# Taking pk^T x over contiguous feature chunks, with z regrouped through memory

## The chip, the cores and the metric

One core of one Trainium2 chip runs the whole program. The metric is the device time of one execution in microseconds (us). Executions of one kernel mostly agree within 1%; much of the scatter comes from the first loads, which let TensorE begin its real work up to some 3 us earlier or later. So beside the whole time I use a stretch that leaves the beginning out: from the start of the first matmul of pk^T x to the end of the last matmul, read from the trace. There is one trace of each kernel.

In the code, `sb(...)` allocates on-chip memory (SBUF), `PS` is the memory that TensorE writes its results to (PSUM), and `nc.dram_tensor` lies in memory outside the core, which the text calls memory. A DMA has landed when its completion is signalled.

## The reference

Two linear-attention blocks A and B work on the same x (2048 x 640, 32 heads of 20 features). A gate mixes their outputs.

```python
def _A_ref(x, wqkv, wo):                 # B is the same with its own weights
    qkv = ...                            # x @ wqkv, split into q, k, v by head
    phi = lambda t: jnp.where(t > 0, t + 1, jnp.exp(t)) + 1e-6
    pq, pk = phi(q), phi(k)
    kv = jnp.einsum("bhsd,bhse->bhde", pk, v)
    z = jnp.einsum("bhsd->bhd", pk)
    num = jnp.einsum("bhqd,bhde->bhqe", pq, kv)
    den = jnp.einsum("bhqd,bhd->bhq", pq, z)[..., None] + 1e-6
    o = num / den
    return ... @ wo
x = A_x
g = _sigmoid((x * gate_w).sum(-1, keepdims=True))
return g * a + (1 - g) * b               # a, b: the two blocks
```

## The kernel before

It never forms v. It computes G = pk^T x, then G wv, masks that to the diagonal blocks of the heads, and folds the result with wo into one matrix per block (WP), which is applied to the scaled pq at the end. z comes from a column of ones that is appended to x: the last column of pk^T [x 1] is the sum of pk over the rows.

Features f are later held in the grouping f = 5 i + k (partition i, group k). To get G and z in that grouping for free, the weights of a matmul of group k are every fifth column of pk:

```python
XW = 642                                  # row length of XN: 640 + the ones column, padded by 1
XN = sb("XN", [128, NT, XW])              # x, row tile t holds rows 128 t to 128 t + 127
...
def g_unit(X, k):                         # X is "A" or "B", k = 0..4
    for t in range(NT):                   # 16 row tiles
        w = PK[X][:, t, k : D : NC]       # stride 5 elements = 10 bytes
        r.append((PS[:, tile.banks[0], 0:HALF], w, XN[:, t, 0:HALF], t == 0, t == NT - 1, None))
        r.append((PS[:, tile.banks[1], 0 : HALF + 1], w, XN[:, t, HALF : D + 1], t == 0, t == NT - 1, None))
    ...
    # z: one column of the second bank, already grouped modulo 5
    e.tensor_copy(Z32[X][:, k : k + 1], PS[:, tile.banks[1], HALF : HALF + 1])
    # G goes to GT by a transposing DMA

def zbd(X):                               # z times the head mask: weights of the denominator
    e.tensor_tensor(out=ZBD[X][:, :, :], in0=<head mask>, in1=Z32[X] broadcast, op=ALU.mult)

def m_unit(X, w):                         # G wv by blocks of 120 columns, then the mask on VectorE
    e.tensor_tensor(
        out=MB[...].rearrange("p q (i k) -> p q k i", k=NC),      # scattered write
        in0=PS[...].rearrange("p (q k i) -> p q k i", ...), in1=<mask>, op=ALU.mult)
...
den: PS[32 rows, 0:256] += ZBD[X][:, k, :] x PQ[X][:, k, ...]     # needs ZBD of A and B, and all pq of the block of rows
```

All instructions are laid out ahead of time by a list scheduler inside the kernel's program. It uses its own estimates of durations and fixes the order of each engine; at run time each engine executes its order and waits where an operand isn't there. For a DMA the estimate is the `us=` argument plus 2 us.

## Time and profile before

| what | value |
|---|---|
| time, median of 3 runs | 200.29 us (199.82 to 201.01) |
| span of the profiled run | 198.6 us |
| TensorE busy, clock | 97%, full throughout |
| first pk^T x matmul to last matmul | 51.60 to 195.55 = 143.95 us |

The first fence holds lines of the page: busy time by engine, then, over 40 equal slices of the span, TensorE's busy tenths and the clock that it was granted. PE is TensorE, PEld its weight loads, DVE VectorE, ACT ScalarE, SP the queue that issues most DMAs.

```profile
span 198.6 us, 3244 instructions
PE 191.7 (97%) x1373; PEld 133.0 (67%) x1379; DVE 105.5 (53%) x201; ACT 79.5 (40%) x124; POOL 6.0 (3%) x16
...
PE   7699999999999999999999999999999999999993
...
PEclk9999999999999999999999999999999999999999
```

TensorE is the bound: it is busy for nine tenths or more of every slice but the first two and the last. Next come groups of instructions by shape: engine, operation, out<-in, count | busy us, mean ns of one | idle before.

```profile
L393 PE MATMUL ps<-XN,FEA 128*128 128x320 bf16 x80 | 22.2, 300 | 0.0
L393 PEld LDWEIGHTS ps<-XN,FEA 128*128 128x128 bf16 x160 | 18.8, 117 | 3.4
...
L393 PEld LDWEIGHTS ps<-WKA,XT 128*128 128x128 bf16 x160 | 15.5, 98 | 5.9
...
L598 DVE TENSOR_TENSOR MB<-ps,CB 120x480 bf16<-120x480 f32 x2 | 3.0, 1507 | 0.1
...
L598 DVE TENSOR_TENSOR MB<-ps,CB 120x120 bf16<-120x120 f32 x2 | 1.2, 583 | 0.0
...
L598 DVE TENSOR_TENSOR MB<-ps,CB 40x40 bf16<-40x40 f32 x2 | 0.5, 261 | 0.1
```

A strided weight load takes 117 ns, a contiguous one 98. The mask (MB) takes about 2.35 us a block (1.51 + 0.58 + 0.26). The table of windows shows how busy each engine is (columns: length; busy us and count of PE, PEld, DVE, ACT, POOL; clock; share of the DMA engines; GB/s), and VectorE's timeline shows z's product:

```profile
107.00:112.00 5.00, 5.00 (x35) 3.01 (x34) 4.60 (x10) 2.89 (x5) 0.00 (x0) 1.00 0.47 168
112.00:118.00 6.00, 5.92 (x62) 3.92 (x61) 5.87 (x11) 3.02 (x6) 0.00 (x0) 1.00 0.00 0
118.00:125.00 7.00, 6.94 (x35) 3.80 (x34) 6.97 (x15) 5.72 (x11) 0.00 (x0) 1.00 0.26 54
```

```profile
100.95 0.15 DVE L552 COPY ZB<-ps 128x1 f32<-128x1 f32 x1
101.13 0.33 DVE L563 TENSOR_TENSOR ZBDB<-CB,ZB 128x160 bf16<-128x160 bf16 x1
```

z of B is complete at 101.1 us and multiplied at once. The first denominator, which needs it, starts at 113.93. VectorE works nearly all the time after that, but TensorE is idle for only 0.14 of these 18 us.

Last, the only DMA of 640 separate small elements (two bytes each) in this trace, the load of the gate vector (issue to landing in us at the end of the line):

```profile
GWC<-in_gate_w_dram SPq DMA_DIRECT2D x1, 1.2 KB, 2.9
```

### The profile page before, as it was taken

To read this page: it belongs to the slowest core of one execution; us is meant where nothing else is said; L and a number is where in the kernel's file an instruction comes from. 1 tells how busy PE (TensorE), PEld (TensorE's weight loads), DVE (VectorE), ACT (ScalarE), POOL (GpSimd) and SP (SyncE) were. 2 spreads that over 40 slices of the span, in tenths; PEclk is the share of its full clock that TensorE was granted. 3 is DMA by queue.
4 is the path that set the end of the run, shared out by engine and by line. 5 is a ranking of instruction groups with operands and counts; after the bars stand their busy time and mean duration, and the time that the engine had idled before them with its cause. 6 is when DMAs were issued, how large, how long until landed. Compare 5 with 4: busy or idle time off the path is not lost.

```text
span 198.6 us, 3244 instructions
## 1 busy us (share of the span) xinstructions
PE 191.7 (97%) x1373; PEld 133.0 (67%) x1379; DVE 105.5 (53%) x201; ACT 79.5 (40%) x124; POOL 6.0 (3%) x16
## 2 busy tenths in 40 slices
PE   7699999999999999999999999999999999999993
PEld 2467777777788877888855655455766665566772
DVE  0359888888600000041159999999405369961400
ACT  2055455455311128302255378545233155514221
POOL 5000000000000000500000000000000000000000
PEclk9999999999999999999999999999999999999999
DMA  6999999990011411111135302440110210011021
GB/s 179 307 232 142 282 348 248 293 224 13 3 33 33 36 33 33 36 33 33 38 80 139 144 0 46 122 165 3 45 54 33 69 61 7 0 36 66 33 69 66
DMA packets 26754, 18.96 MB, mean 95 GB/s; under 512 B 15860, under 2 KB 26484, under 8 KB 26740
## 3 DMA queue, kind: packets, MB, share of 16 engines
q1 hardware_dynamic: 26020, 17.94, 35.5%
q10 hardware_dynamic: 720, 0.82, 1.5%
q8 instruction: 11, 0.18, 0.4%
q14 instruction: 3, 0.02, 0.0%
HBM read 10.89 MB, written 4.26 MB: 76 GB/s over the span
## 4 chain that ended last, share of the span: by engine, by line
PE 93%; DMA 3%; ACT 1%; DVE 1%; issue 1%; SPq 0%
PE ps L393 93%; DMA XN<-in_A_x_dram 3%; DVE FEA L506 0%; SPq L382 0%; PE ps L471 0%; ACT EK L497 0%; ACT OS L808 0%; DVE EK L501 0%
## 5 line engine op out<-in xcount | busy, mean ns | idle before, releaser
L497 ACT ACTIVATE EK<-ps 128x640 bf16<-128x640 f32 x32 | 22.3, 703 | 25.9 <-PE ps L393 25.8
L701 ACT ACTIVATE EK<-ps 128x512 bf16<-128x512 f32 x40 | 23.9, 598 | 19.0 <-PE ps L393 19.0
L808 ACT ACTIVATE OS<-ps 128x640 bf16<-128x640 f32 x16 | 11.2, 703 | 33.0 <-PE ps L393 33.0
L393 PE MATMUL ps<-WPA,FEA 128*128 128x320 bf16 x160 | 24.4, 300 | 0.0
L393 PE MATMUL ps<-WPB,FEB 128*128 128x320 bf16 x160 | 24.3, 299 | 0.0
L393 PE MATMUL ps<-XN,FEB 128*128 128x320 bf16 (+1 forms) x160 | 22.8, 301 | 0.0
L393 PE MATMUL ps<-WKA,XT 128*128 128x320 bf16 x160 | 22.7, 300 | 0.0
L393 PE MATMUL ps<-WKB,XT 128*128 128x320 bf16 x160 | 22.4, 299 | 0.2 <-DVE FEA L506 0.2
L393 PE MATMUL ps<-XT,WQA 128*128 128x512 bf16 x95 | 22.0, 380 | 0.5 <-ACT EK L701 0.2
L393 PE MATMUL ps<-XT,WQB 128*128 128x512 bf16 x99 | 22.4, 380 | 0.1
L393 PE MATMUL ps<-XN,FEA 128*128 128x320 bf16 (+1 forms) x160 | 22.3, 300 | 0.0
L393 PEld LDWEIGHTS ps<-XN,FEB 128*128 128x128 bf16 x160 | 18.6, 118 | 3.7 <-DVE ZA L552 0.4
L393 PEld LDWEIGHTS ps<-XN,FEA 128*128 128x128 bf16 x160 | 18.8, 117 | 3.4
L548 ACT ACTIVATE GS<-ps 128x640 bf16<-128x640 f32 x10 | 7.0, 703 | 34.5 <-PE ps L393 34.5
L393 PEld LDWEIGHTS ps<-WPA,FEA 128*128 128x128 bf16 x160 | 15.3, 98 | 7.1 <-issue 0.9
L393 PEld LDWEIGHTS ps<-WKB,XT 128*128 128x128 bf16 x160 | 15.6, 98 | 6.5 <-issue 0.5
L393 PEld LDWEIGHTS ps<-WPB,FEB 128*128 128x128 bf16 x160 | 15.6, 98 | 6.1
L393 PEld LDWEIGHTS ps<-WKA,XT 128*128 128x128 bf16 x160 | 15.5, 98 | 5.9
L393 PEld LDWEIGHTS ps<-XT,WQB 128*128 128x128 bf16 x100 | 11.6, 117 | 9.6 <-issue 0.2
L393 PEld LDWEIGHTS ps<-XT,WQA 128*128 128x128 bf16 x100 | 11.4, 118 | 9.0 <-issue 0.7
L705 DVE TENSOR_SCALAR EK<-EK 128x512 bf16<-128x512 bf16 x40 | 11.3, 291 | 11.0 <-ACT EK L701 9.7
L501 DVE TENSOR_SCALAR EK<-EK 128x640 bf16<-128x640 bf16 x32 | 10.3, 326 | 7.0 <-ACT EK L497 7.0
(53 smaller groups left out, 145.7 us busy)
## 6 DMA issues: line engine op xcount, KB each, us to landing
out_dram<-OS SPq DMA_DIRECT2D x16, 160.0 KB, 1.8
XN<-in_A_x_dram SPq DMA_DIRECT2D x3, 640.0 KB, 5.8
WKA<-in_A_wqkv_dram ACTq DMA_DIRECT2D x5, 160.0 KB, 4.9
WVA<-in_A_wqkv_dram SPq DMA_DIRECT2D x1, 800.0 KB, 9.1
WQA<-in_A_wqkv_dram SPq DMA_DIRECT2D x1, 800.0 KB, 11.1
WVB<-in_B_wqkv_dram SPq DMA_DIRECT2D x1, 800.0 KB, 15.9
WQB<-in_B_wqkv_dram SPq DMA_DIRECT2D x1, 800.0 KB, 13.4
WPA<-wrowsA SPq DMA_DIRECT2D x1, 800.0 KB, 4.3
```

The costliest lines, as they stand in the source:

```text
L393: ins = pe.matmul(o, l, r, start=a, stop=z, tile_position=tp, skip_group_check=True)
L497: "ACT", lambda e: e.activation(ek2(), pair(tile, HALF), ACT.Exp),
L501: "DVE", lambda e: e.tensor_scalar(ek(), ek(), 1.0, EPS, op0=ALU.min, op1=ALU.add), _dve_ns(D, 4),
L548: "ACT", lambda e: e.activation(GS[:, k, :].rearrange("p (h f) -> p h f", f=HALF), pair(tile, HALF), ACT.Copy),
L701: "ACT", lambda e: e.activation(ek(), PS[:, tile.banks[0], :], ACT.Exp), _act_ns(512), reads=[(tile,)],
L705: "DVE", lambda e: e.tensor_scalar(ek(), ek(), 1.0, EPS, op0=ALU.min, op1=ALU.add), _dve_ns(512, 4),
L808: "ACT", lambda e: e.activation(OS[:, os.slot, :].rearrange("p (h f) -> p h f", f=HALF), pair(tile, HALF), ACT.Copy),
```

## The change

The intent: make the weight loads of pk^T x contiguous (features 128 k to 128 k + 127 instead of every fifth) and with them the mask. G's grouping can be absorbed where GT is read. z's cannot; it is written to memory in natural order and read back in groups of five.

```diff
+        ZN = {X: sb("ZN" + X, [128, NC], dt.float32) for X in XS}
+        ZD = {X: nc.dram_tensor("zrow" + X, [D], dt.float32) for X in XS}
...
-                    w = PK[X][:, t, k : D : NC]
+                    w = PK[X][:, t, 128 * k : 128 * k + 128]
...
-                "DVE", lambda e: e.tensor_copy(Z32[X][:, k : k + 1], PS[...]), 80,
+                "DVE", lambda e: e.tensor_copy(ZN[X][:, k : k + 1], PS[...]), 80,
...
         def zbd(X):
+            zn = ZD[X].ap()
+            dma("SP", "zw" + X, zn.rearrange("(c p) -> p c", p=128), ZN[X][:, :], ..., us=0.6, slow=True)
+            dma("SP", "zr" + X, Z32[X][:, :], zn.rearrange("(i k) -> i k", k=NC), ..., us=0.3, slow=True)
...
-                        out=MB[0:n, ...].rearrange("p q (i k) -> p q k i", k=NC),
-                        in0=PS[...].rearrange("p (q k i) -> p q k i", k=NC, i=w_in), in1=<mask, 4 dimensions>
+                        out=MB[0:n, qq[0] : qq[-1] + 1, 0:n],
+                        in0=PS[...].rearrange("p (q f) -> p q f", f=n), in1=<mask, 3 dimensions>
```

More of the change, by code (lines that the diff above doesn't have):

```diff
@@ L47, in _build_consts @@
     c[:, C_EX : C_EX + 128] = (p % 32)[:, None] == (np.arange(128) // 4)[None, :]
-    c[:, C_MM : C_MM + 120] = (p // DH)[:, None] == ((np.arange(120) % 24) // 4)[None, :]
+    c[:, C_MM : C_MM + 120] = (p // DH)[:, None] == (np.arange(120) // DH)[None, :]
     c[:, C_MH : C_MH + 32] = (p // 4)[:, None] == np.arange(32)[None, :]
@@ L551, in g_unit @@
             sch.op(
-                "DVE", lambda e: e.tensor_copy(Z32[X][:, k : k + 1], PS[:, tile.banks[1], HALF : HALF + 1]), 80,
-                reads=[(tile,)], writes=[("Z", X, k)], name="z%s%d" % (X, k),
+                "DVE", lambda e: e.tensor_copy(ZN[X][:, k : k + 1], PS[:, tile.banks[1], HALF : HALF + 1]), 80,
+                reads=[(tile,)], writes=[("ZN", X, k)], name="z%s%d" % (X, k),
             )
@@ L560, in zbd @@
         def zbd(X):
+            zn = ZD[X].ap()
+            dma(
+                "SP", "zw" + X, zn.rearrange("(c p) -> p c", p=128), ZN[X][:, :], reads=[("ZN", X, k) for k in range(NC)],
+                writes=[("ZD", X)], us=0.6, slow=True,
+            )
+            dma("SP", "zr" + X, Z32[X][:, :], zn.rearrange("(i k) -> i k", k=NC), reads=[("ZD", X)], writes=[("Z", X)], us=0.3, slow=True)
             sch.op(
@@ L566, in zbd @@
                 ),
-                _dve_ns(NC * H), reads=[("Z", X, k) for k in range(NC)] + [("CB",)], writes=[("ZBD", X)], name="zbd" + X,
+                _dve_ns(NC * H), reads=[("Z", X), ("CB",)], writes=[("ZBD", X)], name="zbd" + X,
             )
@@ L582, in steps @@
                             PS[:, tile.banks[0], 120 * (q % 4) : 120 * (q % 4) + NC * wide(q)], WV[X][:, D * j + 120 * q : D * j + 120 * q + 128],
-                            GT[X][:, j, :, 24 * q : 24 * q + wide(q)], j == 0, j == NC - 1, None,
+                            GT[X][:, j, :, :].rearrange("p c f -> p (c f)")[:, 120 * q : 120 * q + NC * wide(q)], j == 0, j == NC - 1, None,
                         ))
@@ L598, in mask @@
                     return e.tensor_tensor(
-                        out=MB[0:n, qq[0] : qq[-1] + 1, 0:n].rearrange("p q (i k) -> p q k i", k=NC),
-                        in0=PS[0:n, tile.banks[0], at : at + n * len(qq)].rearrange("p (q k i) -> p q k i", k=NC, i=w_in),
-                        in1=CB[0:n, C_MM : C_MM + 120].rearrange("p (k i) -> p k i", i=24)[:, :, 0:w_in].unsqueeze(1).to_broadcast(
-                            [n, len(qq), NC, w_in]
-                        ),
-                        op=ALU.mult,
+                        out=MB[0:n, qq[0] : qq[-1] + 1, 0:n],
+                        in0=PS[0:n, tile.banks[0], at : at + n * len(qq)].rearrange("p (q f) -> p q f", f=n),
+                        in1=CB[0:n, C_MM : C_MM + n].unsqueeze(1).to_broadcast([n, len(qq), n]), op=ALU.mult,
                     )
```

## The prediction

> **What bounds the kernel now.** TensorE: 97% of 198.6 us on the page's busy line, 93% of the chain of waits, at full clock. VectorE is 53% busy, but the table of windows shows it saturated just after pk^T x: 10.9 of 13 us (100 to 113), 6.96 of 7, 10.7 of 11 (to 131). TensorE is still idle for only 0.5 us there.
>
> **Removed.** (a) The 320 weight loads of pk^T x read every fifth bf16 and take 117 ns; contiguous ones (WK,XT) take 98 (groups by shape). 6 us of load time should go, but it is hidden: the Trainium skill ("TensorE: Matmul & The Clock Gate", step by step) says that the next weights load while this matmul runs, and the trace agrees: loads of 117 ns fit inside a spacing of about 136.
>
> Yet the stage's matmuls are 138.4 ns apart on average, those of the K and output stages with 320 columns 135.9: 320 x 2.5 = 0.8 us. The single spacings, in order of row tile t, have period four: t = 0, 4, 8, 12 take 135 to 136, the others 138 to 141. The weights cannot do that: rows of pk are 1,280 bytes, a multiple of 16, with one stride throughout. The moving operand can: rows of XN are 1,284 bytes, so only every fourth begins on 16 bytes. "SBUF — State Buffer" (the door on the port swizzle) gives SBUF 16-byte lines; the period fits. XN stays, so I expect the 0.8 us to stay. Not excluded: unaligned operand and slow load cost only together; then up to 0.8 us goes.
>
> (b) The mask on VectorE: 1.50 + 0.58 + 0.26 us a branch. Contiguous, by the slope of other PSUM reads (512 columns 0.69, 640 columns 0.825 us), I estimate 0.65 + 0.28 + 0.19, so 1.2 us less a branch. A's lies where VectorE is idle, B's (113 us) where it is saturated; TensorE's idle time there bounds its worth to 0.3 us.
>
> **Added.** Four DMAs: 640 four-byte elements a branch to memory and back. The gate vector's load of 640 elements took 2.9 us from issue to landing; I estimate 2.5 to 4 us out, 2 to 3 back. A: from 74.7 us, needed at 113.9: slack. B: z is complete at 101.1; its write is issued near 102, competes with the 750 KB store of folded weights (landed 107.7), and is back near 107 to 109; the denominator needs it at 113.9. No direct cost. Indirectly: each engine's order is fixed; if VectorE reaches the product with the head mask before z is back, it stalls up to 1.5 us just before its saturated stretch. The shorter mask pays 1.2 back.
>
> **Moved.** m's matmuls: same number, columns, spacing. The list scheduler may reorder: half a microsecond either way.
>
> **Sum.** Loads 0, mask -0.2, stalls +0.1, order 0: 200.2 us; 8 in 10 within 199.1 to 201.5. Chances: faster by over 2% 0.01, within 2% 0.96, slower by over 2% 0.03.
>
> **Right or wrong.** Weight loads of XN,FE fall from 117 to 98 ns; spacing there keeps its period of four and mean of 138; the stage stays 22 us a branch. MB groups fall to about 0.65, 0.28, 0.19 us. ZBDB starts near 108, not 101, before the denominator near 114. TensorE stays 97% busy.
>
> **What would make it wrong.** A write of z of over 8 us, so that VectorE or the denominator waits; the period of four vanishing (0.8 us faster); a reordering that starves the PSUM banks.

## The result, and the profile after

The changed kernel takes 207.28 us (median of 6 runs, 205.84 to 208.04), the kernel before 200.06 us (6 runs). The ratio is 1.0343, 95% interval 1.0281 to 1.0404: 3.4% slower. Ratios are the mean time of one kernel's fast runs over the mean of the other's of the same rounds, so they aren't quite the ratio of the medians quoted.

The same lines of the page, with the chain of work that ended last:

```profile
span 203.7 us, 3254 instructions
PE 194.1 (95%) x1379; PEld 127.5 (63%) x1379; DVE 103.3 (51%) x201; ACT 79.6 (39%) x124; POOL 6.0 (3%) x16
...
PE   7999999999999999999999099999999999999994
...
PEclk9999999999999999999999769999999999999999
...
PE 86%; DMA 9%; DVE 2%; ACT 1%; SPq 0%; issue 0%
PE ps L395 86%; DMA zrowB<-ZNB 5%; DMA XN<-in_A_x_dram 2%; DMA ZB<-zrowB 2%; DVE FEB L716 1%; DVE FEA L508 0%; DVE EK L711 0%; SPq L384 0%; PE ps L473 0%; ACT EK L499 0%; ACT OS L814 0%; ACT EK L707 0%; DVE EK L503 0%; DVE ZBDB L572 0%
```

One slice has TensorE at 0, and just there and in the next one the clock drops to 7 and 6 tenths. The chain passes through B's two new DMAs, 5% and 2% of the span. The groups show that the intended savings are there, and a new wait at ZBDB and ZBDA (A's is harmless: VectorE waits for it until 85.6 us, and TensorE doesn't pause there):

```profile
L395 PE MATMUL ps<-XN,FEA 128*128 128x320 bf16 x80 | 22.1, 299 | 0.0
L395 PEld LDWEIGHTS ps<-XN,FEA 128*128 128x128 bf16 x160 | 15.6, 98 | 6.5
...
L607 DVE TENSOR_TENSOR MB<-ps,CB 120x480 bf16<-120x480 f32 x2 | 1.3, 647 | 0.0
...
L572 DVE TENSOR_TENSOR ZBDB<-CB,ZB 128x160 bf16<-128x160 bf16 x1 | 0.3, 326 | 6.0 <-DMA ZB<-zrowB 6.0
L572 DVE TENSOR_TENSOR ZBDA<-CB,ZA 128x160 bf16<-128x160 bf16 x1 | 0.3, 325 | 6.8 <-DMA ZA<-zrowA 6.8
```

The DMA issues (KB, us from issue to landing) of the round trip:

```profile
zrowA<-ZNA SPq DMA_DIRECT2D x1, 2.5 KB, 8.7
ZA<-zrowA SPq DMA_DIRECT2D x1, 2.5 KB, 2.8
zrowB<-ZNB SPq DMA_DIRECT2D x1, 2.5 KB, 10.1
ZB<-zrowB SPq DMA_DIRECT2D x1, 2.5 KB, 3.2
```

The writes take 8.7 and 10.1 us, not 2.5 to 4. The timelines of VectorE and of TensorE show what B's write does (start, length, engine, what; in brackets the idle time before it and what ended it):

```profile
107.40 0.69 DVE L716 SCALAR_TENSOR_TENSOR FEB<-ps,EK 128x512 bf16<-128x512 f32 x1
114.14 0.33 DVE L572 TENSOR_TENSOR ZBDB<-CB,ZB 128x160 bf16<-128x160 bf16 x1 [6.05 <-DMA ZB<-zrowB]
114.38 0.29 DVE L711 TENSOR_SCALAR EK<-EK 128x512 bf16<-128x512 bf16 x1
...
116.55 0.69 DVE L716 SCALAR_TENSOR_TENSOR FEB<-ps,EK 128x512 bf16<-128x512 f32 x1
```

```profile
110.92 1.25 PE L395 MATMUL ps<-XT,WQA 128*128 128x512 bf16 x5
117.30 0.40 PE L395 MATMUL ps<-FEA,ZBDA 128*32 128x256 bf16 x2 [5.12 <-DVE FEB L716]
```

VectorE reaches the product ZBDB at 108.09 and stands there for 6.05 us. Three pairs of instructions that make pq of B (FEB) stand behind it in VectorE's fixed order, though they don't need z. TensorE's next instruction, the first denominator, needs the last of them and pauses for 5.12 us. The windows complete it:

```profile
107.00:112.00 5.00, 5.00 (x48) 3.20 (x46) 1.00 (x3) 1.83 (x4) 0.00 (x0) 1.00 0.00 0
112.00:118.00 6.00, 0.88 (x17) 0.56 (x20) 3.75 (x9) 0.60 (x1) 0.00 (x0) 0.68 0.40 137
118.00:125.00 7.00, 7.00 (x39) 3.54 (x32) 5.33 (x11) 4.05 (x7) 0.00 (x0) 0.78 0.01 2
```

Two things are to be seen. From 107 to 112 us the DMA share rounds to 0.00 although the write is still out: in the DMA's packet records its last packet ends at 105.79, and it lands 5.1 us later, at 110.88. And the clock is below full in the last two windows. The trace's clock record says half speed from 114.22 us for 6.83 us; the matmuls agree with it, those of q with 512 columns start 427 ns apart before 121.04 and 215 ns apart after it. All six runs of the changed kernel had a mean clock below full, 0.981 to 0.992.

The loss adds up. From the first pk^T x matmul to the last matmul the changed kernel takes 150.80 us, 6.85 more than before. The pause is 5.12. From 117.30 to 121.04 TensorE works at half speed, 3.74 us, which loses 1.87. Together 6.99, which agrees with 6.85 within the scatter of this stretch.

### The profile page after: what moved, and what is told of

It reads as the page before. It is cut to its first block, busy times and chain, and to the rows that moved or that the text cites. A ratio compares the mean times of both kernels' runs of the same rounds, so it can differ in the third digit from the quotient of the medians.

```text
span 203.7 us, 3254 instructions
## 1 busy us (share of the span) xinstructions
PE 194.1 (95%) x1379; PEld 127.5 (63%) x1379; DVE 103.3 (51%) x201; ACT 79.6 (39%) x124; POOL 6.0 (3%) x16
## 4 chain that ended last, share of the span: by engine, by line
PE 86%; DMA 9%; DVE 2%; ACT 1%; SPq 0%; issue 0%
PE ps L395 86%; DMA zrowB<-ZNB 5%; DMA XN<-in_A_x_dram 2%; DMA ZB<-zrowB 2%; DVE FEB L716 1%; DVE FEA L508 0%; DVE EK L711 0%; SPq L384 0%; PE ps L473 0%; ACT EK L499 0%; ACT OS L814 0%; ACT EK L707 0%; DVE EK L503 0%; DVE ZBDB L572 0%
## 5 line engine op out<-in xcount | busy, mean ns | idle before, releaser
L395 PE MATMUL ps<-XT,WQA 128*128 128x512 bf16 x100 | 24.1, 392 | 0.0
L395 PEld LDWEIGHTS ps<-XN,FEA 128*128 128x128 bf16 x160 | 15.6, 98 | 6.5
L395 PEld LDWEIGHTS ps<-XN,FEB 128*128 128x128 bf16 x160 | 15.5, 98 | 6.7 <-DVE ZNA L554 0.4
L503 DVE TENSOR_SCALAR EK<-EK 128x640 bf16<-128x640 bf16 x32 | 10.4, 329 | 6.9 <-ACT EK L499 6.8
```

The source lines that it names most:

```text
L395: ins = pe.matmul(o, l, r, start=a, stop=z, tile_position=tp, skip_group_check=True)
L503: "DVE", lambda e: e.tensor_scalar(ek(), ek(), 1.0, EPS, op0=ALU.min, op1=ALU.add), _dve_ns(D, 4),
```

## The experiments

The theory after the result: the whole loss is z's write landing late, by way of VectorE's fixed order, TensorE's pause and the clock. Rivals: the new loads or the new mask cost something; small writes cost this much anywhere; the denominator would wait in any order; the clock drop does no harm.

**1. The change without the round trip.** The head mask takes z in its natural grouping. Its output is wrong, which doesn't matter for the time. (The comparison with the reference doesn't see z's grouping.) Apart from the missing DMAs and the place of the head-mask products, the order of every engine is that of the changed kernel, and it is the same as before's.

```diff
-            dma("SP", "zw" + X, ...)
-            dma("SP", "zr" + X, ...)
-                    in1=Z32[X][:, :].unsqueeze(2).to_broadcast([128, NC, H]), op=ALU.mult,
+                    in1=ZN[X][:, :].unsqueeze(2).to_broadcast([128, NC, H]), op=ALU.mult,
```

> The change without the memory round trip: the head mask is multiplied with z as it stands, in the wrong grouping, so the result is wrong on purpose. TensorE, ScalarE keep the order of both kernels. Theory T1 (the whole loss is the round trip of z: VectorE waits for it, TensorE for VectorE, and the clock drops in the pause): 199.5 to 200.5 us, no pause of TensorE over 0.5 us, clock 1.00, weight loads of pk^T x 98 ns, matmul spacing there still 138 ns with period four, so within 0.5% of before. Rival T2 (contiguous loads or the new mask layout cost something themselves): stays above 203 us. Rival T3 (the contiguous loads are worth 0.8 us, the round trip ate them): 199.2 us or less.

Measured: 199.73 us against 199.14 for before on the same chip, ratio 1.0033 (1.0000 to 1.0067). (Before took 200.06 us beside the changed kernel, so ratios are compared and not times in us.) In the trace no pause after the first loads, loads of 98 ns, mean spacing in pk^T x 138.14 ns with the period of four. The stretch from the first pk^T x matmul is 143.83 us against before's 143.95. T1 holds; T2 and T3 fall. The 0.12 us between the stretches is within their scatter: shorter loads and the shorter mask together are worth nothing that the runs can tell.

**2. The kernel before with aligned rows of x.** This tests the reading on which I denied the weight loads any worth.

```diff
-XW = 642
+XW = 648
```

> The kernel before with one number changed: rows of XN are 648 instead of 642 elements, 1,296 bytes, a multiple of 16; weight loads stay strided (117 ns). Theory (the 2.5 ns a matmul come from the moving operand's alignment): all spacings in pk^T x become 135 to 136 ns, the stage loses 320 x 2.5 = 0.8 us in all, the time falls to 199.3 us. Rival (they come from the strided weights, or from something else that has period four): the period stays, time as before.

Measured: 198.36 us against 199.14, ratio 0.9969 (0.9944 to 0.9994). These are the start-to-start distances in ns of the 32 matmuls of A's first group, two for each row tile t = 0 to 15, worked out from the trace's records:

```
before, 642:  136 137  140 139  139 139  139 139 | 135 136  139 139  138 140  138 140 | 135 136  140 140  138 140  138 141 | 136 135  139 139  139 140  138 140
changed, 642: 136 137  140 139  138 139  139 139 | 135 136  140 139  138 139  139 140 | 135 136  139 140  138 139  138 140 | 135 136  139 140  138 140  138 140
this, 648:    136 137  136 136  136 137  136 136 | 136 137  136 136  136 137  136 136 | 136 137  136 136  136 137  136 136 | 136 137  136 136  136 137  136 136
```

With 1,284-byte rows only every fourth tile begins on a multiple of 16 bytes, and only those tiles run at 136. The changed kernel has the same pattern, with loads of 98 ns instead of 117. With 1,296-byte rows the pattern is gone, with loads still of 117 ns. So the theory holds: the period of four came from the moving operand's alignment. It accounts for 2.1 of the 2.5 ns a matmul (mean spacing 138.35 before, 136.26 here; about 135.9 in the K and output stages, whose matmuls all have 320 columns, while half of these have 321). The stretch falls from 143.95 to 143.30, 0.65 us, a little less than the 0.8 expected.

**3 and 4. z's elements far apart in memory.** The same 640 four-byte writes, to addresses 512 or 64 bytes apart. The order is that of the changed kernel.

```diff
-        ZD = {X: nc.dram_tensor("zrow" + X, [D], dt.float32) for X in XS}
+        ZD = {X: nc.dram_tensor("zrow" + X, [D, 128], dt.float32) for X in XS}      # run 4: [D, 16]
-... zn.rearrange("(c p) -> p c", p=128)
+... zn.rearrange("(c p) s -> p c s", p=128)[:, :, 0]
-... zn.rearrange("(i k) -> i k", k=NC)
+... zn.rearrange("(i k) s -> i k s", k=NC)[:, :, 0]
```

> The changed kernel with z's 640 elements 512 bytes apart in memory instead of 4; the same 640 four-byte writes, but the read back is 640 four-byte pieces rather than 128 of 20 bytes. Same order of instructions. Theory W1 (the 7 us between the last packet of the write, 75.7, and its landing, 82.8, come from writes to neighbouring addresses waiting for one another): the write of A lands in 2.5 to 3.5 us instead of 8.7, that of B in under 6, TensorE's pause shrinks to under 1 us, clock 1.00, 200 to 201 us. Rival W2 (each small write costs, wherever it goes): landing stays 8 us or more and the time near 207.

> As the run with 512 bytes between elements, but 64. If W1 holds with a contended unit of at most 64 bytes: the same as with 512 bytes, 200 to 201 us. If the contended unit is larger (512 bytes hold eight elements then, not 128): the write of A lands in between, 3.5 to 6 us. If W2: no difference between 4, 64 and 512 bytes, near 207 us.

Measured: 200.37 us, ratio 1.0042 (1.0002 to 1.0081) at 512 bytes; 199.39 us, ratio 1.0014 (0.9985 to 1.0042) at 64 bytes. Both stretches are 143.83 us, as without a round trip, though the interval at 512 bytes lies just above 1. The DMA issues of the run with 64 bytes, and VectorE's line:

```profile
zrowA<-ZNA SPq DMA_DIRECT2D x1, 2.5 KB, 2.2
ZA<-zrowA SPq DMA_DIRECT2D x1, 2.5 KB, 2.3
zrowB<-ZNB SPq DMA_DIRECT2D x1, 2.5 KB, 5.6
ZB<-zrowB SPq DMA_DIRECT2D x1, 2.5 KB, 2.2
```

```profile
108.88 0.33 DVE L572 TENSOR_TENSOR ZBDB<-CB,ZB 128x160 bf16<-128x160 bf16 x1 [0.49 <-DMA ZB<-zrowB]
```

The number, size and order of the writes are those of the changed kernel; only their distance differs, and A's write falls from 8.7 to 2.2 us. W1 holds and W2 falls. (At 512 bytes it takes 2.35 us, a little under the expected 2.5 to 3.5.) The packet records show where the time goes: A's packets leave within 1 us in both kernels, but from the last packet to the landing it is 7.1 us in the changed kernel (75.72 to 82.81) and 0.7 us here (76.02 to 76.69). VectorE's wait shrinks from 6.05 to 0.49 us and the pause is gone. B's write still takes 5.6 us. It is issued just after the 750 KB store of the folded weights, on the same queue, and its four-byte packets leave among the store's 1,280-byte packets until 106.07, 5.0 us after the issue; it lands 0.6 us after that. So the store accounts for this time by the trace, though no run moved the store away.

**5. The slow write, but the scheduler knows.** Nothing is faster here; the scheduler's estimate alone is changed.

```diff
-                writes=[("ZD", X)], us=0.6, slow=True,
+                writes=[("ZD", X)], us=7.5, slow=True,
```

> The changed kernel, z written as slowly as in it (four bytes apart), but the scheduler's estimate for that write is raised from 0.6 to 7.5 us, so VectorE meets the product with the head mask some six instructions later and TensorE the first denominator later. Theory O (a slow write costs only because the fixed order puts its reader too early): the write of B still lands only after 8 us or more, yet TensorE's longest pause is under 1 us, clock 1.00, 199.5 to 201 us. Rival D (whatever the order, the denominator's need of z comes before z is back): a pause of 2 us or more, 202 us or more.

Measured: 200.00 us, ratio 1.0056 (0.9984 to 1.0128). B's write takes 10.4 us and z is back at 115.01, 0.9 us later than in the changed kernel, yet the stretch is 143.81 us, without a pause. (In the profiled run the clock is full; another of the four runs took 201.95 us at a mean clock of 0.991, and where its clock dropped isn't known.)

```profile
zrowB<-ZNB SPq DMA_DIRECT2D x1, 2.5 KB, 10.4
```

```profile
115.18 0.32 DVE L572 TENSOR_TENSOR ZBDB<-CB,ZB 128x160 bf16<-128x160 bf16 x1
...
115.87 0.29 PE L395 MATMUL ps<-FEB,ZBDB 128*32 128x256 bf16 x2
```

VectorE meets the product twelve instructions later (about six were expected), after the pq instructions and B's mask, and finds z ready; TensorE folds some weights and does some q first and starts the denominator at 115.87. O holds, D falls: here the slow write was harmless once the fixed order allowed for it. The order moved the product on VectorE and the denominator on TensorE together; which of the two would have sufficed isn't shown.

**6. Work in the pause.** The slow write and the early product as in the changed kernel, with 20 matmuls, whose results nobody uses, before the pause.

```diff
+            if b == 0:
+                mms("fill", lambda: [(PS[:, dtile.banks[0], :], WQ["A"][:, 0, 0:128], XT[:, 0, 0:512], True, True, None)] * 20, [],
+                    [(dtile,)], 0, after=next(o for o in sch.ops if o.name == "eqB04"))
             mms("den%d" % b, den, ...)
```

> The changed kernel with 20 matmuls of 512 columns (4.3 us, their results overwritten unused) put into TensorE's stream just before its pause. Nothing waits less: VectorE's order and z's way stay. Theory C (of the 7 us lost, 5.1 are the pause and about 1.9 the half clock that the pause brings on): clock stays 1.00, the pause shrinks to about 1 us, the denominator starts as late as before (TensorE's work after it unshifted), and the time falls by 1.9 us, to 1.9 below the changed kernel's 206 to 207, a ratio to before of about 1.025. Rival (the clock drop costs nothing on the way, because other engines bound that stretch): same time as the changed kernel, ratio 1.034.

Measured: 204.36 us, ratio 1.0249 (1.0197 to 1.0300). The windows that answer to those above:

```profile
112.00:118.00 6.00, 5.31 (x51) 2.67 (x49) 3.73 (x9) 0.60 (x1) 0.00 (x0) 1.00 0.38 137
118.00:125.00 7.00, 7.00 (x40) 4.19 (x37) 6.90 (x15) 5.79 (x11) 0.00 (x0) 1.00 0.01 2
```

```profile
114.17 0.32 DVE L572 TENSOR_TENSOR ZBDB<-CB,ZB 128x160 bf16<-128x160 bf16 x1 [5.93 <-DMA ZB<-zrowB]
...
117.33 0.29 PE L395 MATMUL ps<-FEA,ZBDA 128*32 128x256 bf16 x2 [0.69 <-DVE FEB L716]
```

VectorE waits 5.93 us as before, the denominator starts at 117.33 instead of 117.30, TensorE's pause is 0.69 us, and the clock stays full, here and in the other three runs. The stretch is 148.91 us, 1.89 less than the changed kernel's 150.80. C holds: the two terms of the loss are 5.1 and 1.9 us. (The whole times alone wouldn't quite separate the two kernels: their intervals, from 1.0281 and up to 1.0300, just overlap.)

**7. Everything that helped, together.** Contiguous loads, z 64 bytes apart, rows of 648 elements (the edits of runs 2 and 4 on the changed kernel).

> Contiguous weight loads, z 64 bytes apart in memory, and rows of XN of 648 elements: all that helped, together. Theory (contiguous loads are worth nothing even once the moving operand is aligned): the same as the kernel before with 648 alone, ratio 0.997 within 0.3%, spacing 136.3 in pk^T x. Rival (with aligned rows the shorter loads now show): spacing under 136.0 and a ratio below 0.994.

Measured: 198.90 us against 198.97, ratio 0.9980 (0.9937 to 1.0023); spacing 136.25 ns against run 2's 136.26; stretch 143.23 us against 143.30. Even with aligned rows, contiguous loads are worth nothing that the runs can tell. Run 2, one number changed in the kernel before, is the only version whose interval lies wholly below 1, by 0.3%; this version isn't shown to be faster than before.

**8. How far apart is enough?** Distances of 8, 16 and 32 bytes.

```diff
-        ZD = ... [D, 16] ...
+        ZD = ... [D, 8] ...        # 32 bytes; [D, 4]: 16; [D, 2]: 8
```

> One look: z's elements 32 bytes apart in memory. Theory W1 with a contended unit of 64 bytes: two elements share one, so the write of A lands a little later than the 2.2 us with 64 bytes, 2.3 to 3 us. If the unit is 32 bytes or less: 2.2 us.

> One look: z's elements 16 bytes apart in memory. Under W1 with a unit of 64 bytes four elements share one: the write of A lands in 2.8 to 4.5 us. If the unit is 16 bytes or less: 2.2 us. If the time goes with the whole stretch of memory rather than with sharing: in proportion between 4 and 64 bytes, near 5 us.

> One look: z's elements 8 bytes apart in memory. Under W1 with a unit of 64 bytes eight elements share one: the write of A lands in 4 to 6.5 us, about half way between 2.2 (64 bytes apart) and 8.7 (4 bytes apart); TensorE's pause shrinks to 0 to 3 us.

| distance, bytes | write of A, us | write of B, us | VectorE waits before B's product | TensorE's pause |
|---|---|---|---|---|
| 4 (changed kernel) | 8.66 | 10.11 | 6.05 | 5.12 |
| 8 | 4.31 | 7.37 | 2.3 | 1.42 |
| 16 | 3.05 | 6.08 | 1.0 | none over 0.2 |
| 32 | 2.15 | 5.45 | 1.0 | none |
| 64 | 2.24 | 5.56 | 0.49 | none |
| 512 | 2.35 | 5.36 | 0.3 | none |

At 32 bytes the cost is gone, so the unit that is shared is not 64 bytes in size, or two sharers cost too little to see. At 8 and 16 bytes the landing lies in the ranges expected of sharing; a cost in proportion to the stretch of memory would have given near 5 us at 16. The whole times of these single runs (202.53, 201.76 and 203.59 us at 32, 16 and 8 bytes) are of unknown state and blurred by the first loads: pk^T x began at 53.5, 52.6 and 53.5 us in them, against 49.9 in the changed kernel. Their stretches are 143.96, 144.00 and 145.32 us. The last is 1.5 us above 143.83, about its pause of 1.42 alone: after this shorter pause the clock stayed full.

## Why the prediction was right or wrong

- *TensorE bounds the kernel.* Right; that is why its pause of 5.12 us comes out in full.
- *Weight loads 117 to 98 ns, hidden, worth 0.* Right. The loads take 98 ns, the spacing stays (138.35 to 138.17 ns), and run 1 finds no gain of loads and mask together beyond the scatter of the stretch. The Trainium skill's statement that the next weights load during this matmul ("TensorE: Matmul & The Clock Gate", step by step) agrees with it.
- *The period of four comes from rows of 1,284 bytes.* Right, shown by run 2: the period is gone, 136.26 ns and ratio 0.9969 once rows are a multiple of 16 bytes. The size came out at 0.65 us of the stretch, not 0.8.
- *Mask 0.65 + 0.28 + 0.19 us.* Right: 0.647, 0.271, 0.192. That little of it reaches TensorE fits run 1.
- *"I estimate 2.5 to 4 us out, 2 to 3 back."* This step failed. Out it took 8.7 us (A) and 10.1 us (B), back 2.8 and 3.2. I sized a write from the load of the gate vector, 640 elements in 2.9 us. That load reads memory and writes SBUF. The z write puts 640 four-byte pieces on neighbouring addresses in memory, and runs 3, 4 and 8 show that it is the neighbourhood that costs: 2.2 to 2.4 us (A) when they are 32 bytes or more apart.
- *"it stalls up to 1.5 us"*, *"back near 107 to 109"*, *"No direct cost."* These follow from the failed size. z came back at 114.11; VectorE stood for 6.05 us; the denominator began at 117.30 instead of near 114. With z 64 bytes apart (run 4), B's z was back 7.8 us after its write was issued, where the prediction had 5 to 7, and the wait was 0.49 us: with a write near the forecast size the rest of this reasoning holds. The chain of events was the one named (the product with the head mask in VectorE's fixed order), and the list of what would make the prediction wrong even begins with a write of over 8 us. But it got no weight in the range, and one term was missing altogether: a pause of this length halves the clock afterwards, another 1.9 us (run 6). "stalls +0.1" in the sum measured 7.0.

What stays open: what inside the memory path makes neighbouring small writes wait for one another, and how large the shared unit is.

## What to carry to other kernels

Price a DMA from one with the same direction and the same pattern; here a store of 640 scattered elements to neighbouring addresses took 8.6 to 10.4 us, and the load of the gate vector's 640 took 2.9 to 4.6 in these traces. Keeping the stored elements 32 bytes apart was enough here. In a kernel whose order is fixed ahead, and which has other work to do meanwhile, a transfer needs an honest estimate more than speed: the same slow write cost 7 us with a wrong one and nothing that the runs can tell with a right one. Before shortening weight loads, look at the spacing of single matmuls: loads that fit inside the spacing were worth nothing here, and a pattern in the spacing can point to the operand that does cost.

## What the Trainium skill lacked or had wrong

- "DMA: Bandwidth & Descriptors", the anatomy of one DMA, gives about 2.0 us fixed for a DMA issued by GpSimd, most of it the write receipt, and quotes that it can be surprisingly long into HBM. z's writes are issued by SP; 64 bytes apart, A's takes about as long (2.24 us). It lacks that neighbouring small writes multiply it: 8.66 us at 4 bytes, 4.31 at 8, 3.05 at 16, 2.15 at 32.
- The same page, specifications, says that transfers under 512 bytes are done by read-modify-write. Size alone doesn't explain these runs: the same four-byte writes land in 2.35 us at 512 bytes' distance, in 2.15 at 32 and in 8.66 at 4. The page says nothing of the distance.
- "SBUF — State Buffer", the door on the port swizzle, has 16-byte lines and speaks of strides. It lacks the start of a matmul's moving operand: a row off a multiple of 16 bytes costs about 3 ns on a spacing of 136 at 320 columns (139 on average), 0.65 us here.
- "TensorE: Matmul & The Clock Gate", part 1, puts the return to half clock after an idle window of about 3.4 us. Here the half clock came 2.05 us after the last matmul's end in the trace (112.17 to 114.22) and lasted 6.83 us. In the twelve traces all changes of the clock within a trace lie whole multiples of 3.41 us apart. Counted in such pieces of 3.41 us, one in which TensorE was idle for 1.80 us kept the full clock (before, 4.91 to 8.33), and those with 2.04 (the changed kernel, 110.80 to 114.22), 2.06 and 2.08 us (the first loads at 8 and 32 bytes) lost it at their end: such a piece needn't be idle throughout. The page gives no such share.
- The same page, on weight loads, gives columns over 1.2, which is 107 ns for 128, and of fast weight load it says that the chunks may be packed or strided, and gives no difference in time for the two. The trace has 98 ns contiguous and 117 at a stride of 10 bytes; whether fast weight load was on isn't shown.
